# Loading q and k in runs of 18 tokens, sending five batches through DRAM rows, and reordering the front of a fused attention and MLP kernel

## The chip, the cores and the metric

The kernel runs on one core of one Trainium2 chip. The metric is the device time of one execution in microseconds, the lowest being best. Most executions of one kernel agree within some 0.3%, and some fall in a slower state; a run over 1.5% above the fastest of its kernel is called slow.

## The reference

Eight batches of eight heads attend within a window of 32 tokens to either side; the result, as 4608 tokens of 512 values, goes through two matrix products with an ELU between them.

```python
B, H, S, D = 8, 8, 576, 64
scores = (q @ k.T) / sqrt(D);  masked where |i - j| > 32
attn   = softmax(scores);      x = (attn @ v) as [B*S, H*D]     # 4608 x 512
h = x @ w_in                                                    # 512 x 2048
g = where(h > 0, h, exp(min(h, 0)) - 1)
out = g @ w_out                                                 # 2048 x 512, f32
```

## The kernel before

The MLP is cut into 18 tiles of 256 tokens with 8 steps each, 144 steps in all. A step is eight first-layer products, an exp on ScalarE, two VectorE operations, and, two steps later, four second-layer products. The attention of 36 pairs of query blocks is spread between these steps as tasks: pair i is computed some steps before the tile that needs it. The products of the scores take q and k with the head dimension on partitions; so each batch is loaded as f32, cast to bf16 and transposed.

```python
def load_qk(b, which, part):              # rows of 6 tokens a partition: 96 partitions
    ...
    nc.sync.dma_start(out=t[...].rearrange("p (h x) -> p h x", h=H),
                      in_=(q, k)[which][b, :, ...].rearrange("h (p j) d -> p h (j d)", j=nj))

def rotate_v(b, m0=0, m1=VS - 1):         # the copy of V shifted by 64 tokens: DMA
    nc.sync.dma_start(out=o[0:64, m0:m1], in_=e[64:128, m0:m1])
    nc.sync.dma_start(out=o[64:128, m0:m1], in_=e[0:64, m0 + 1:m1 + 1])

def transpose_rows(b, which):             # bf16 rows written to DRAM, read back transposed
    nc.sync.dma_start_transpose(out=keys_or_queries(b, which), in_=in_dram.pop((b, which)))

def x_dma(i):                             # attention result of pair i, transposed by DMA
    nc.sync.dma_start_transpose(out=xT_of(i), in_=x_st.rearrange("p h d -> p (h d)"))

# the plan, for batches 2 to 7 (k0: step at which the batch's first pair begins)
for b in range(2, B):
    k0 = begin[first_pair(b)]
    if b >= 3:
        kk = max(k0 - 26 if b < 5 else k0 - 36, 18)
        at(kk, "mid", load_qk, b, 0, WHOLE)
        at(kk + 1, "mid", load_qk, b, 1, WHOLE)
        ...                               # loads of V from step kk + 2
    if b < 5:                             # casts on GpSimd, transposes on TensorE
        for n in range(2 * HP):
            ...
            at(kk - 2 - b // 3, "mid", cast_qk, b, which, WHOLE, (hp,), nc.gpsimd)
            at(kk, "mid", transpose_qk, b, which, WHOLE, (hp,), nc.scalar)
    else:                                 # casts on ScalarE, rows through DRAM
        ...
        at(c0 + 6, "mid", write_rows, b, which)
        at(c0 + 9, "mid", transpose_rows, b, which)
    at(k0 - HALF, "mid", rotate_v, b)
```

SyncE issues its transfers in program order. In one queue stand the loads of q and k, the DMA transposes of the rows in DRAM, the DMA transposes of x, which the first-layer products wait for, and the stores of the result.

The softmax here doesn't subtract the row's maximum and nothing guards it: scores larger than these inputs give would overflow.

## Time and profile before

| | before |
|---|---|
| median of its first 3 runs | 337.37 us (336.4 to 337.61) |
| span of the profiled execution (slow) | 340.9 us |
| TensorE busy | 307.2 us, 90% |
| first MLP product starts | 26.3 us |
| GpSimd's casts of batch 2, VectorE stretched beside them | around 68 us |

The page of a profile gives busy time by engine and in forty slices of the span. The timeline lists start, length and, in brackets, the idle time ahead with what ended it. The prediction shows the lines.

### The profile page before, as it was taken

To read this page: it belongs to the slowest core of one execution; us is meant where nothing else is said; L and a number is where in the kernel's file an instruction comes from. 1 tells how busy PE (TensorE), PEld (TensorE's weight loads), DVE (VectorE), ACT (ScalarE), POOL (GpSimd) and SP (SyncE) were. 2 spreads that over 40 slices of the span, in tenths; PEclk is the share of its full clock that TensorE was granted. 3 is DMA by queue.
4 is the path that set the end of the run, shared out by engine and by line. 5 is a ranking of instruction groups with operands and counts; after the bars stand their busy time and mean duration, and the time that the engine had idled before them with its cause. 6 is when DMAs were issued, how large, how long until landed. Compare 5 with 4: busy or idle time off the path is not lost.

```text
span 340.9 us, 7736 instructions
## 1 busy us (share of the span) xinstructions
PE 307.2 (90%) x3152; PEld 203.3 (60%) x3152; DVE 239.8 (70%) x446; ACT 171.8 (50%) x262; POOL 63.4 (19%) x84
## 2 busy tenths in 40 slices
PE   0358999789899999899999999799999999999994
PEld 0245666456566666566666666556666666666661
DVE  4445667577786779676877778377777787877663
ACT  1624264555556634587646666446645444434431
POOL 8352310094461129110011100000000000000000
PEclk9999999899999999999999999979999999999998
DMA  8999999999999999918999999969590420202011
GB/s 174 183 231 219 216 164 200 211 228 228 148 149 169 234 198 188 174 67 165 221 250 176 203 245 158 215 104 223 95 200 18 139 74 22 77 17 80 0 62 62
DMA packets 93862, 52.72 MB, mean 155 GB/s; under 512 B 67908, under 2 KB 87364, under 8 KB 93828
## 3 DMA queue, kind: packets, MB, share of 16 engines
q1 hardware_dynamic: 51428, 39.79, 55.8%
q0 software_dynamic: 41728, 8.92, 38.9%
q10 hardware_dynamic: 672, 3.54, 3.4%
q8 instruction: 24, 0.39, 0.5%
q14 instruction: 10, 0.08, 0.1%
HBM read 36.70 MB, written 12.98 MB: 146 GB/s over the span
## 4 chain that ended last, share of the span: by engine, by line
PE 74%; DMA 12%; DVE 8%; ACT 3%; issue 1%; SPq 0%; DVEq 0%
PE ps L489 34%; PE psY L516 31%; DMA xT<-x_st 8%; PE psS L312 3%; PE psS L284 3%; PE ptx L265 3%; DMA f<-in_k_dram 2%; DVE g_sb L502 2%; DVE m_sb L497 2%; ACT e_sb L495 2%; DMA Vo<-Ve 2%; DVE x_st L324 1%; ACT qkb L211 1%; DVE pm L300 1%; ACT pu L291 1%
## 5 line engine op out<-in xcount | busy, mean ns | idle before, releaser
L495 ACT ACTIVATE e_sb<-ps 128x512 f32<-128x512 f32 x144 | 86.0, 597 | 148.4 <-PE ps L489 146.4
L489 PE MATMUL ps<-xT,w_in_sb 128*128 128x256 bf16 x1152 | 153.1, 277 | 5.8 <-DVE xT L346 3.7
L516 PE MATMUL psY<-w_out_sb,g_sb 128*128 128x512 bf16 x576 | 149.7, 383 | 0.9 <-DVE g_sb L502 0.9
L489 PEld LDWEIGHTS <-w_in_sb 128*128 128x128 bf16 x1152 | 111.3, 99 | 44.6 <-issue 6.7
L502 DVE SCALAR_TENSOR_TENSOR g_sb<-ps,m_sb 128x512 bf16<-128x512 f32 x144 | 99.3, 690 | 13.8 <-DVE m_sb L497 0.5
L497 DVE TENSOR_SCALAR m_sb<-e_sb 128x512 bf16<-128x512 f32 x144 | 66.0, 459 | 60.2 <-ACT e_sb L495 58.7
L516 PEld LDWEIGHTS <-g_sb 128*128 128x128 bf16 x576 | 52.9, 98 | 39.8 <-DVE g_sb L502 1.5
L123 POOL DMA_DIRECT2D Ve<-in_v_dram x40 | 34.1, 858 | 94.5 <-PE psS L312 81.0
L291 ACT ACTIVATE pu<-psS 128x1024 bf16<-128x1024 f32 x36 | 36.5, 1019 | 3.2 <-PE psS L284 3.1
L265 PE MATMUL ptx<-ident,qkb 96*128 96x96 bf16 x240 | 17.7, 221 | 14.4 <-DVE qkb L213 12.0
L324 DVE TENSOR_TENSOR x_st<-psS,rc 128x512 bf16<-128x512 f32 x36 | 24.9, 691 | 6.4 <-DMA xT<-x_st 5.2
L300 DVE TENSOR_TENSOR pm<-pu,masks 128x1024 bf16<-128x1024 bf16 x36 | 26.4, 733 | 2.0 <-ACT pu L291 1.7
L213 POOL CAST qkb<-f 96x768 bf16<-96x768 f32 x24 | 20.8, 901 | 31.6 <-DMA f<-in_q_dram 22.0
L265 PEld LDWEIGHTS <-qkb 96*128 96x128 bf16 x240 | 14.5, 106 | 16.4 <-DVE qkb L213 12.5
L312 PEld LDWEIGHTS <-pm 128*64 128x64 bf16 x576 | 12.8, 115 | 17.0 <-DVE pm L300 11.4
L243 ACT CAST rows<-f 96x768 bf16<-96x768 f32 x24 | 19.7, 822 | 0.0
L284 PE MATMUL psS<-qT,kT 64*128 64x64 bf16 x576 | 15.3, 196 | 3.2 <-DVE x_st L324 1.8
L284 PEld LDWEIGHTS <-kT 64*128 64x128 bf16 x576 | 11.2, 98 | 10.7 <-issue 7.3
L312 PE MATMUL psS<-Vo,pm 128*64 128x65 bf16 x256 | 14.8, 203 | 2.6 <-DMA Vo<-Ve 1.8
L312 PE MATMUL psS<-Ve,pm 128*64 128x65 bf16 x320 | 16.8, 202 | 0.0
L211 ACT COPY qT<-ptx 128x576 bf16<-128x576 bf16 (+1 forms) x18 | 12.4, 689 | 4.1 <-PE ptx L265 4.1
L525 DVE COPY y_sb<-psY 128x512 f32<-128x512 f32 x18 | 12.3, 683 | 2.8 <-PE psY L516 2.8
(29 smaller groups left out, 64.3 us busy)
## 6 DMA issues: line engine op xcount, KB each, us to landing
out_dram<-y_sb SPq DMA_DIRECT2D x18, 512.0 KB, 3.4
f<-in_q_dram SPq DMA_DIRECT2D x6, 1152.0 KB, 12.7
f<-in_k_dram SPq DMA_DIRECT2D x6, 1152.0 KB, 15.9
in_dram<-rows ACTq DMA_DIRECT2D x6, 576.0 KB, 4.2
Vo<-Ve SPq DMA_DIRECT2D x12, 260.0 KB, 5.3
Ve<-in_v_dram POOLq DMA_DIRECT2D x24, 128.0 KB, 13.2
f<-in_q_dram SPq DMA_DIRECT2D x4, 576.0 KB, 9.7
f<-in_k_dram SPq DMA_DIRECT2D x4, 576.0 KB, 11.7
```

What stands on the lines that cost most here:

```text
L123: nc.gpsimd.dma_start(out=V_e[b % 3][p0:p1, m, :, 0:D], in_=v[b, :, lo + p0:lo + p1, :].rearrange("h p d -> p h d"))
L265: nc.tensor.transpose(pt[:, g, j * SP_:(j + 1) * SP_], src[:, j, g * 128:(g + 1) * 128], ident[0:SP_, 0:SP_])
L284: nc.tensor.matmul(psS[:, h % 2, hp * 128 + z * QB:hp * 128 + (z + 1) * QB], lhsT=kT[b % 2][base:base + 64, KPAD + hp * S + QB * qb - WIN: ...
L291: nc.scalar.activation(pu, _bap(psS, [psS.ap[0], [1, 1024]]), AX.Exp, scale=SCALE)
L300: nc.vector.tensor_mul(pm, pu, _bap(mm, [mm.ap[0], [0, H], [1, 2 * QB]]))
L312: nc.tensor.matmul(psS[QB * z:QB * (z + 1), par, hp * VD:(hp + 1) * VD], lhsT=pm[:, par * HP + hp, z * QB:(z + 1) * QB], rhs=vv[:, qb // 2 ...
L324: nc.vector.tensor_mul(x_st, _bap(psS, [psS.ap[0], [VD, HP], [512, 2], [1, D]]), _bap(rc, [rc.ap[0], [2, HP], [1, 2], [0, D]]))
L489: nc.tensor.matmul(ps[:, j, :], lhsT=w_in_sb[:, do, fo * 128:(fo + 1) * 128], rhs=xT[t][:, :, do, :], start=(do == 0), stop=(do == NDO - 1))
L495: nc.scalar.activation(e_sb, ps, AX.Exp)
L497: nc.vector.tensor_scalar(m_sb, e_sb, -1.0, None, ALU.add)
L502: nc.vector.scalar_tensor_tensor(g_sb, psH.pop(kk), 0.0, m_t.pop(kk), ALU.max, ALU.min)
L516: nc.tensor.matmul(psY[t][ts], lhsT=g_sb[:, j, ts * 128:(ts + 1) * 128], rhs=w_out_sb[:, s * FG + j, :], start=(s == 0 and j == 0), stop=( ...
```

## The change

Its intent: longer contiguous rows for q and k (18 tokens, or 9 in the front, on 128 partitions), so fewer packets in those loads; batches 3 and 4 through DRAM too, so 96 transposes fewer on TensorE; no casts on GpSimd; the shifted copy of V by VectorE instead of DMA; a quicker front, with products of zeros in TensorE's waits to keep its clock up. The core of the diff, with cuts marked:

```diff
     def load_qk(b, which, part):
...
+        src = (q, k)[which][b, :, z * NC * nj:(z + 1) * NC * nj, :].rearrange(
+            "(g h) (c j) d -> c g h (j d)", h=2, j=nj)
+        for h in range(2):
+            nc.sync.dma_start(out=t[:, h, :], in_=src[:, :, h, :])
...
-        nc.sync.dma_start(out=o[0:64, m0:m1], in_=e[64:128, m0:m1])
-        nc.sync.dma_start(out=o[64:128, m0:m1], in_=e[0:64, m0 + 1:m1 + 1])
+        nc.vector.tensor_copy(o[0:64, m0:m1], e[64:128, m0:m1])
+        nc.vector.tensor_copy(o[64:128, m0:m1], e[0:64, m0 + 1:m1 + 1])
...
+    def idle(n, tag):
+        ps = ps_tile([128, 512], FP32, tag, "ps_idle")
+        for _ in range(n):
+            nc.tensor.matmul(ps, lhsT=zeros[:, 0:128], rhs=zeros,
+                             start=True, stop=True)
...
+    idle(12, "y1")
+    front_cast(0, HALF_A, nc.vector)
+    front_transpose(0, HALF_A, nc.scalar, ("h0", "h1"))
+    idle(5, "u")
+    front_cast(1, HALF_A, nc.scalar)
+    front_transpose(1, HALF_A, nc.vector, ("y0", "y1"))
     for i, tag in ((0, "s"), (1, "u")):
         scores(i, tag)
+    idle(8, "h1")
...
-    pair_at(4, 10)
-    pair_at(5, 13)
+    pair_at(4, 9)
+    pair_at(5, 12)
...
-            kk = max(k0 - 26 if b < 5 else k0 - 36, 18)
+            kk = max(k0 - 30, 18)
             at(kk, "mid", load_qk, b, 0, WHOLE)
             at(kk + 1, "mid", load_qk, b, 1, WHOLE)
...
-        if b < 5:
-            ...                              # casts on GpSimd, transposes on TensorE
+        if b == 2:
+            free = [f for f in range(17, k0) if f not in starts]
+            ...                              # casts on ScalarE, transposes on TensorE
         else:
+            free = [f for f in range(k0 - LEAD, k0) if f not in starts]     # LEAD = 18
+            for n, (which, j0) in enumerate(groups):
+                at(free[n], "end", cast_qk, b, which, WHOLE, j0, 6, nc.scalar)
+                if j0 == 12:
+                    at(free[n], "end", write_rows, b, which)
+                    at(free[n] + 4, "mid", transpose_rows, b, which)
-        at(k0 - HALF, "mid", rotate_v, b)
+        at(k0 - HALF - 1, "dve", rotate_v, b)
```

More of the change, by code (lines that the diff above doesn't have):

```diff
@@ L44 @@
     HP = H // 2
-    SJ = 6
-    SP_ = S // SJ
+    NC = 128 // HP
+    SJ = S // NC
     VS = 5
@@ L108, in load_qk @@
         z, nj = part
-        if (b, which) not in qk_f:
-            qk_f[b, which] = lpool.tile([SP_, H * SJ * D], FP32,
-                                        tag=f"f{which}", name=f"f{which}")
-        t = qk_f[b, which]
-        n = H * nj * D
-        nc.sync.dma_start(
-            out=t[:, z * n:(z + 1) * n].rearrange("p (h x) -> p h x", h=H),
-            in_=(q, k)[which][b, :, z * SP_ * nj:(z + 1) * SP_ * nj, :]
-            .rearrange("h (p j) d -> p h (j d)", j=nj))
+        t = lpool.tile([128, 2, nj * D], FP32, tag=f"f{which}{nj}",
+                       name=f"f{which}")
+        qk_f[b, which, z] = t
+        src = (q, k)[which][b, :, z * NC * nj:(z + 1) * NC * nj, :].rearrange(
+            "(g h) (c j) d -> c g h (j d)", h=2, j=nj)
+        for h in range(2):
+            nc.sync.dma_start(out=t[:, h, :], in_=src[:, :, h, :])
     def load_v(b, m):
@@ L155, in w_in_at @@
         return w_in_sb[0:1, 0, (c + 1) * (D_FF // 4) - 1:(c + 1) * (D_FF // 4)]
+    zeros = cpool.tile([128, 512], BF16, name="zeros")
+    nc.vector.memset(zeros, 0.0)
     for i in range(3):
@@ L171 @@
             load_qk(0, which, part)
-    for m in (1, 2, 0, 3, 4):
+    for m in (1, 0, 2, 3, 4):
         load_v(0, m)
-    rotate_v(0, 0, 2)
-    rotate_v(0, 2, VS - 1)
     load_w_in(0)
@@ L213, in copy_on, with cast_qk @@
             eng.tensor_copy(d_, s_)
-    def cast_qk(b, which, part, hps, eng):
+    def cast_qk(b, which, part, j0, n, eng):
         z, nj = part
-        hp0, nh = hps[0], 2 * len(hps)
-        n = H * nj * D
-        s_ = qk_f[b, which][:, z * n + 2 * hp0 * nj * D:
-                            z * n + (2 * hp0 + nh) * nj * D]
-        s_ = _bap(s_, [s_.ap[0], [nj * D, nh], [D, nj], [1, D]])
-        t = lpool.tile([SP_, nj, nh * D], BF16, tag=f"b{which}", name="qkb",
-                       bufs=4)
-        qk_b[b, which, z, hp0] = t
-        copy_on(eng, _bap(t, [t.ap[0], [D, nh], [nh * D, nj], [1, D]]), s_)
+        if (b, which, z) not in qk_b:
+            qk_b[b, which, z] = lpool.tile(
+                [128, nj, 2 * D], BF16, tag=f"b{which}{nj}", name="qkb")
+        t = qk_b[b, which, z]
+        copy_on(eng,
+                t[:, j0:j0 + n, :].rearrange("p j (h d) -> p h j d", h=2),
+                qk_f[b, which, z][:, :, j0 * D:(j0 + n) * D].rearrange(
+                    "p h (j d) -> p h j d", d=D))
     def keys_or_queries(b, which):
         if which == 0:
-            return qT[b % 2]
-        return kT[b % 2][:, KPAD:KPAD + HP * S].rearrange(
-            "p (g s) -> p g s", g=HP)
-    rows, in_dram = {}, {}
-    def cast_rows(b, which, hp):
-        if hp == 0:
-            rows[b, which] = lpool.tile([SP_, SJ, H * D], BF16,
-                                        tag=f"r{which}", name="rows", bufs=1)
-        n = SJ * D
-        s_ = qk_f[b, which][:, 2 * hp * n:(2 * hp + 2) * n]
-        d_ = rows[b, which][:, :, 2 * hp * D:(2 * hp + 2) * D]
-        nc.scalar.copy(
-            _bap(d_, [d_.ap[0], [D, 2], [H * D, SJ], [1, D]]),
-            _bap(s_, [s_.ap[0], [n, 2], [D, SJ], [1, D]]))
+            return qT[b % 2].rearrange("p g s -> p (g s)")
+        return kT[b % 2][:, KPAD:KPAD + HP * S]
+    in_dram = {}
     def write_rows(b, which):
-        t = dpool.tile([S, H * D], BF16, tag=f"d{which}", name="in_dram")
+        t = dpool.tile([HP * S, 2 * D], BF16, tag=f"d{which}", name="in_dram")
         in_dram[b, which] = t
         nc.scalar.dma_start(
-            out=t.rearrange("(p j) c -> p j c", j=SJ), in_=rows.pop((b, which)))
+            out=t.rearrange("(g c j) x -> c g (j x)", g=HP, j=SJ),
+            in_=qk_b.pop((b, which, 0)).rearrange("p j x -> p (j x)"))
     def transpose_rows(b, which):
@@ L255, in transpose_rows, with transpose_qk @@
             out=keys_or_queries(b, which), in_=in_dram.pop((b, which)))
-    def transpose_qk(b, which, part, hps, evac, tag="t0"):
+    def transpose_qk(b, which, part, j0, n, evac, tag="t0"):
         z, nj = part
-        src = qk_b.pop((b, which, z, hps[0]))
-        nh = len(hps)
-        W = 512 if nh > 1 else 1024
-        pt = ps_tile([128, nh, W], BF16, tag, "ptx")
-        for g in range(nh):
-            for j in range(nj):
-                nc.tensor.transpose(
-                    pt[:, g, j * SP_:(j + 1) * SP_],
-                    src[:, j, g * 128:(g + 1) * 128], ident[0:SP_, 0:SP_])
-        n = SP_ * nj
-        d = keys_or_queries(b, which)[:, hps[0]:hps[0] + nh, z * n:(z + 1) * n]
-        pitch = d.ap[1][0] if nh > 1 else n
+        src = qk_b[b, which, z]
+        pt = ps_tile([128, 1024 if n <= 8 else 2048], BF16, tag, "ptx")
+        for j in range(n):
+            nc.tensor.transpose(
+                pt[:, j * 128:(j + 1) * 128], src[:, j0 + j, :], ident)
+        d = keys_or_queries(b, which)
         copy_on(evac,
-                _bap(d, [d.ap[0], [pitch, nh], [nj, SP_], [1, nj]]),
-                _bap(pt, [pt.ap[0], [W, nh], [1, SP_], [SP_, nj]]))
+                _bap(d, [d.ap[0], [S, HP], [nj, NC], [1, n]],
+                     z * NC * nj + j0),
+                _bap(pt, [pt.ap[0], [1, HP], [HP, NC], [128, n]]))
     st = {}
@@ L343, in xT_of, with x_evac @@
         return xT[t][:, z, :, :]
-    def x_evac(i):
-        nc.vector.tensor_copy(xT_of(i), st.pop(i))
+    def x_evac(i, eng=nc.vector):
+        copy_on(eng, xT_of(i), st.pop(i))
     def x_dma(i):
@@ L354, in first_pair, with front_cast, front_transpose @@
         return NQB * b // 2
-    warm = cpool.tile([128, 1], FP32)
-    nc.vector.memset(warm, 0.0)
-    nc.scalar.activation(warm, warm, AX.Exp)
-    def front_qk(part, tags):
-        for g in range(2):
-            hps = (2 * g, 2 * g + 1)
-            cast_qk(0, 0, part, hps, nc.vector)
-            cast_qk(0, 1, part, hps, nc.scalar)
-            transpose_qk(0, 0, part, hps, nc.scalar, tags[g])
-            transpose_qk(0, 1, part, hps, nc.vector, tags[2 + g])
-    front_qk(HALF_A, ("h0", "h1", "y0", "y1"))
+    SPLIT = ((0, 5), (5, 4))
+    def front_cast(which, part, eng):
+        for j0, n in SPLIT:
+            cast_qk(0, which, part, j0, n, eng)
+    def front_transpose(which, part, evac, tags):
+        for (j0, n), tag in zip(SPLIT, tags):
+            transpose_qk(0, which, part, j0, n, evac, tag)
+    def idle(n, tag):
[3 more added lines that the diff above has]
+                             start=True, stop=True)
+    warm = cpool.tile([128, 1], FP32)
+    nc.scalar.activation(warm, zeros[:, 0:1], AX.Exp)
+    idle(12, "y1")
[4 more added lines that the diff above has]
+    front_transpose(1, HALF_A, nc.vector, ("y0", "y1"))
     for i, tag in ((0, "s"), (1, "u")):
         scores(i, tag)
+    idle(8, "h1")
+    front_cast(0, HALF_B, nc.vector)
+    front_transpose(0, HALF_B, nc.scalar, ("h0", "h1"))
     for i in (0, 1):
         mask(i)
-    front_qk(HALF_B, ("h0", "h1", "y0", "y1"))
-    for fn in (pv, normalize, x_transpose, x_evac):
-        for i in (0, 1):
-            fn(i)
+    front_cast(1, HALF_B, nc.scalar)
+    idle(4, "y1")
+    front_transpose(1, HALF_B, nc.scalar, ("y0", "y1"))
+    rotate_v(0, 0, 2)
+    idle(4, "h1")
+    for i in (0, 1):
+        pv(i)
+    for i in (0, 1):
+        normalize(i)
+    rotate_v(0, 2, VS - 1)
+    idle(4, "h1")
+    for i in (0, 1):
+        x_transpose(i)
+    for i in (0, 1):
+        x_evac(i, nc.scalar)
     gate(w_out_sb[0:1, NFO // 4 - 1, D_MODEL - 1:D_MODEL])
@@ L386 @@
         load_w_out(c)
-    rotate_v(1, 0, 2)
     gate(w_in_at(3))
@@ L392 @@
         load_v(1, m)
-    rotate_v(1, 2, VS - 1)
     for which in range(2):
@@ L422 @@
         at(1, "dve", mask, i)
-        at(1, "mid", pv, i)
+        at(1, "end", pv, i)
         at(2, "dve", normalize, i)
         at(2, "mid", x_transpose, i)
-        at(3, "dve", x_evac, i)
+        at(2, "end", x_evac, i, nc.scalar)
     at(4, "dve", swap_pools)
-    allh = tuple(range(HP))
     for part, kq in ((HALF_A, 8), (HALF_B, 16)):
         for which in range(2):
-            at(kq - 1, "mid", cast_qk, 1, which, part, allh,
+            at(kq - 1, "mid", cast_qk, 1, which, part, 0, SJ // 2,
                (nc.scalar, nc.vector)[which])
-            at(kq + which, "mid", transpose_qk, 1, which, part, allh,
+            at(kq + which, "mid", transpose_qk, 1, which, part, 0, SJ // 2,
                nc.scalar, "s")
-    pair_at(4, 10)
-    pair_at(5, 13)
+    at(10, "dve", rotate_v, 1, 0, 2)
+    at(17, "dve", rotate_v, 1, 2, VS - 1)
+    pair_at(4, 9)
+    pair_at(5, 12)
     pair_at(6, 18)
@@ L449 @@
         at(kk + 2, "end", x_dma, i)
+    starts = set(begin.values()) | {9, 12, 18}
+    LEAD = 18
     for b in range(2, B):
@@ L457 @@
                 at(kk + 2 + m // 3, "mid", load_v, b, m)
-        if b < 5:
-            for n in range(2 * HP):
-                which, hp = n // HP, n % HP
-                kk = k0 - (8 if b == 2 else 10) + n
-                at(kk - 2 - b // 3, "mid", cast_qk, b, which, WHOLE, (hp,),
-                   nc.gpsimd)
-                at(kk, "mid", transpose_qk, b, which, WHOLE, (hp,), nc.scalar)
-        else:
-            for which in range(2):
-                c0 = k0 - 27 + 8 * which
-                for hp in range(HP):
-                    at(c0 + (0, 1, 4, 5)[hp], "end", cast_rows, b, which, hp)
-                at(c0 + 6, "mid", write_rows, b, which)
-                at(c0 + 9, "mid", transpose_rows, b, which)
-        at(k0 - HALF, "mid", rotate_v, b)
+        groups = [(which, j0) for which in range(2) for j0 in (0, 6, 12)]
+        if b == 2:
+            free = [f for f in range(17, k0) if f not in starts]
+            for n, (which, j0) in enumerate(groups):
+                at(free[max(n - 1, 0)], "end", cast_qk, b, which, WHOLE, j0,
+                   6, nc.scalar)
+                at(free[n + 1], "mid", transpose_qk, b, which, WHOLE, j0,
+                   6, nc.scalar)
+        else:
+            free = [f for f in range(k0 - LEAD, k0) if f not in starts]
+            for n, (which, j0) in enumerate(groups):
+                at(free[n], "end", cast_qk, b, which, WHOLE, j0, 6, nc.scalar)
[3 more added lines that the diff above has]
+        at(k0 - HALF - 1, "dve", rotate_v, b)
     order = [(z, n) for z in range(2) for n in range(HALF)]
```

## The prediction

> **What bounds the kernel now.** I read the core's clock (0.987, one core, so no die to compare), then the page's busy shares and slices, then the timeline of the front, then TensorE's waits in windows of 10 us, then the queue of SyncE. The shares come first:
>
> ```profile
> PE 307.2 (90%) x3152; PEld 203.3 (60%) x3152; DVE 239.8 (70%) x446; ACT 171.8 (50%) x262; POOL 63.4 (19%) x84
> PE   0358999789899999899999999799999999999994
> ```
>
> TensorE is the bound, except in slices 1 to 4 (the front), slice 8 (60 to 68 us) and slice 27 (about 222 us). So there are two questions: what work leaves TensorE, and which holes close. The pace where nothing disturbs it, from the timeline near the end:
>
> ```profile
> 316.49 1.04 PE L489 MATMUL ps<-xT,w_in_sb 128*128 128x256 bf16 x8
> 318.23 1.04 PE L489 MATMUL ps<-xT,w_in_sb 128*128 128x256 bf16 x8
> ```
>
> One step (8 products of 256 columns, 4 of 512) starts every 1.737 us. From 230.91 to 238.79 us lie four steps and one attention pair: 7.88 - 4 x 1.737 = 0.93 us per pair. The chain of waits gives a group of six q/k transposes 0.26 us, so 43 ns each. My ledger of the span: front 26.3; 144 x 1.737 = 250.1; 34 pairs after the front x 0.93 = 31.6; 192 transposes after the front, about 9; transposes of x, 1.5; tail after the last product 340.9 - 336.15 = 4.75. Sum 323.3, so about 17.6 us of the 340.9 are holes. The front:
>
> ```profile
> 8.42 0.83 ACT L211 CAST qkb<-f 96x768 bf16<-96x768 f32 x1 [2.33 <-DMA f<-in_k_dram]
> ...
> 22.68 0.26 PE L312 MATMUL psS<-Vo,pm 128*64 128x65 bf16 x1 [1.84 <-DMA Vo<-Ve]
> ...
> 26.32 1.87 PE L489 MATMUL ps<-xT,w_in_sb 128*128 128x256 bf16 x8 [0.52 <-DVE xT L346]
> ...
> 29.09 1.89 PE L489 MATMUL ps<-xT,w_in_sb 128*128 128x256 bf16 x8
> ```
>
> See that k lands at 8.4 us, that the shifted copy of V, a DMA of 5.6 us, releases the second products at 22.68, and that the first MLP products take 1.87 us for the 0.87 of the steady state. The second-layer products begin at 34.99 (8.67 us later, of which only 4.5 is work, so 4.1 lost). Then slice 8:
>
> ```profile
> 64.50 1.03 PE L489 MATMUL ps<-xT,w_in_sb 128*128 128x256 bf16 x8 [1.86 <-DVE xT L346]
> 65.88 1.84 PE L516 MATMUL psY<-w_out_sb,g_sb 128*128 128x512 bf16 x4
> 67.51 1.91 PE L489 MATMUL ps<-xT,w_in_sb 128*128 128x256 bf16 x8
> 68.33 3.32 POOL L213 CAST qkb<-f 96x768 bf16<-96x768 f32 x4 [22.01 <-DMA f<-in_q_dram]
> 71.66 1.03 PE L489 MATMUL ps<-xT,w_in_sb 128*128 128x256 bf16 x8 [0.83 <-ACT y_sb L524]
> 73.36 1.04 DVE L497 TENSOR_SCALAR m_sb<-e_sb 128x512 bf16<-128x512 f32 x1 [1.20 <-ACT e_sb L495]
> ```
>
> A wait for xT behind VectorE's cast, then half pace, then GpSimd's casts with VectorE's 0.43 us operation stretched to 1.04. Counting products in windows, 60 to 90 us loses 6.3 us. SyncE's queue explains slice 27:
>
> ```profile
> 199.01 14.68 SPq L254 DMA_TRANSPOSE qT<-in_dram  x1
> 213.79 4.94 SPq L350 DMA_TRANSPOSE xT<-x_st  x2
> ```
>
> A DMA transpose issued right behind 2.4 MB of loads held the queue for 14.68 us; the transposes of x came behind it, and VectorE and TensorE waited (about 4 us lost; a like wait at 141 us cost 1.2). Named holes: 4.1 + 6.3 + 4 + 1.2 = 15.6.
>
> The profiled run took 343.73 us and is marked slow; 343.73 - 340.9 = 2.8 lies outside the span, so a usual run of 337.37 has a span near 334.5, 6.4 shorter. I choose to read the two waits behind DMA transposes (5.2 us) as mostly absent from usual runs; the trace can't prove it.
>
> **What the Trainium skill says.** (1) "TensorE: Matmul & The Clock Gate", the part on the clock gate: after an idle window of about 3.4 us the array runs at half clock until a busy one. The trace agrees in effect: 1.87 against 0.87 us behind the gappy front and after the hole at 62 us. The same page's part on PE-mode transpose says that transposes don't count as busy; no run here shows that yet. (2) "SBUF — State Buffer", Who interferes with whom: VectorE's two-port modes and GpSimd lock each other out. The trace agrees: 0.43 to 1.04 us. (3) "VectorE: DVE Perf Modes", the perf-mode tier table: a bf16 copy within SBUF runs at 4x, 693 ns for 2048 elements. The trace has no such copy yet; its f32 casts (560 ns for 768, 951 for 1536) have a slope of 0.51 ns an element, which is the 2x of that table. (4) "Perfetto Trace Analysis", DMA Optimizations: transfers under 2 KB have significant overhead each. Here 87364 of 93862 packets are under 2 KB; pieces of q and k are 768 or 1536 bytes before, 2304 or 4608 after.
>
> **The change part by part.**
>
> Loads. q and k of the first batch are 4 x 768 packets before, 4 x 256 after. They ran near 220 GB/s (2.36 MB from about 2 to 12 us); I take 350 for the longer rows, as the best slices of the later 1536-byte loads show 340 to 390. So q lands by 4.5, k by 6, the second halves by 9, and V, which ran mostly after them, by about 13 for its first three blocks instead of 16.4.
>
> Front, by the durations above, estimated on each engine's order. VectorE's fills end at 6.3 us (a zero tile of about 0.49 is added to the 5.85), q casts 0.49 + 0.43 to 7.3, its copies out on ScalarE 0.70 + 0.58 to 8.55, k casts 0.72 + 0.60 to 9.9, k's copies out on VectorE to 11.2, scores to 11.95, two exps to 13.6. Second halves on ScalarE: copies out 1.3, k casts 1.3, to 16.7; k's transposes to 16.95; four zero products 0.86 to 17.8; weighted V 0.86 to 18.7; the shifted V is now two VectorE copies of about 0.44 and is ready by 15.3. Normalising, transposing and copying x ends near 21.2. First MLP product at 21.2 instead of 26.3: **-5.1**. Zero products run in waits and should keep the clock up.
>
> First steps. At full clock the first three steps reach the second layer after about 7.3 us instead of 8.67 (exp, mask and normalise of pairs 2 and 3 still make it wait): **-1.4**.
>
> Transposes. Batches 3 and 4 go through DRAM: 96 transposes x 43 to 50 ns leave a TensorE-bound stretch: **-4.5**. Batches 1 and 2: 96 x 43 = 4.1 us become 72 of 128 columns, 72 x 57 = 4.1: nothing.
>
> Slice 8. GpSimd's 24 casts (20.8 us) go to ScalarE, which frees VectorE of the stretching, and pair 5 comes a step earlier, so xT is there in time: the 6.3 go. What comes: scores of pair 4 directly behind k's copy out in the same step, about 1.3; the 0.83 wait for y stays; ScalarE in steps 17 to 26 carries six casts and six copies of about 0.83, 1.0 us a step on top of 1.0, against TensorE's 2.25, so it is near full: 1.0 for jams. Net **-3.2**.
>
> Shifted V: 2 copies of 2080 elements x (693/2048) ns = 0.70 each, per batch 1.4 us in VectorE's emptiest step. VectorE gains 11 us in all and loses 7 of stretching; two steps of slack in the products hide it: 0.
>
> DRAM rows. Ten DMA transposes instead of six. The one that frightens me is q of batch 3: in program order it stands with the load of k of batch 4 just ahead of the transpose of x of pair 9, which is needed three steps later. Before, that transpose took 4.1 us of some 5 available. Behind an issue of 3 to 5 us and 1.2 MB more it must be late; 4 to 5 us of waiting and some half clock could follow. Later pairs have seven or eight steps of slack. I count **+3.5**.
>
> Sum: -5.1 - 1.4 - 4.5 - 3.2 + 3.5 = -10.7, so 326.7. By the new ledger: 21.2 + 250.1 + 31.6 + 4.1 + 1.5 + 4.75 = 313.3, holes 2.8 + 1.3 + 0.8 + 1.0 + 3.5 = 9.4, outside 2.8, so 325.5. I predict **325.5 us**.
>
> **The rivals.** (a) The queue of transposes bites: each DRAM transpose holds SyncE as at 199 us, and x comes late again and again: +8 to +12, some 335. For it: the 14.68. Against: the loads have a third of the packets and stand 16 steps ahead. (b) The weights become the front's bound: the first w_in quarter landed near 20.3 us and the second near 26.9, and the new order wants them at 21.2 and 25.9; if the small packets of V keep their pace, half of the front's gain turns into a wait: 328 to 330. (c) Batch 2's casts now stand in ScalarE's order eight us earlier than the data used to land (68.3); SyncE no longer waits for V in between, so I expect it near 55, but if not, exps stop behind the cast: +3 to +5. (d) No late x at all and a quicker front: 319 to 321.
>
> **Range and chances.** The gains of TensorE's own work and of the front are fairly firm (6 to 12 together); holes are not, by 4 either way. Range 318.5 to 332.5. 2% is 330.6: faster 0.80, within 2% 0.17, slower 0.03.
>
> **What would show it.** The first MLP product near 21 us, lasting about 1 us and not 1.87; GpSimd without casts and the 128x512 operation never above 0.6 us; 108 transposes on TensorE; VectorE copies of V near 0.7 us; a wait of the products on xT about step 32. I am wrong if the first product starts after 24 us, if V copies take 2 us, or if SyncE holds DRAM transposes over 10 us more than once.

## More of the kernel before

One view it didn't show is SyncE's queue around the transposes of x of pairs 8 and 9 in the kernel before:

```profile
95.38 8.59 SPq L350 DMA_TRANSPOSE xT<-x_st  x2
104.07 0.54 SPq L114 DMA_DIRECT2D f<-in_q_dram  x1
```

Here the load of q comes after those two transposes of x.

## The result, and the profile after

The changed kernel took 342.95 us (median of four runs, 342.27 to 343.44), the kernel before on the same chip 337.49 (336.4 to 338.02). The ratio is 1.0165, with a 95% interval from 1.0134 to 1.0195. Ratios here are the mean time of one kernel's fast runs over that of the other's in the same rounds, so not quite the ratio of the medians quoted. It is slower by 1.65%: clear of the noise, less than the 2% of the verdicts here ("same"), and outside the predicted range.

The page after, busy shares, slices and granted clock:

```profile
PE 309.8 (91%) x3057; PEld 199.3 (59%) x3057; DVE 243.0 (71%) x460; ACT 174.4 (51%) x262; POOL 43.3 (13%) x60
PE   7677989998963999999799999999999999999994
PEclk9799999999995999999799999999999999999999
```

Counted from 1, slices 1 to 4 are busier (partly with products of zeros) and slice 8 is 9 now. But there are two new holes: slices 12 and 13 (94 to 111 us) and slice 20 (162 to 170), and in slices 13 and 20 (and 2, in the front) the clock falls. The waits of TensorE on transfers name them (in total, times, longest, in us):

```profile
PE ps L501 <- DMA xT<-x_st: 9.7, 2, 9.3
PE psS L265 <- DMA kT<-in_dram: 2.2, 1, 2.2
```

The timeline of TensorE at both places:

```profile
108.10 1.89 PE L501 MATMUL ps<-xT,w_in_sb 128*128 128x256 bf16 x8 [9.28 <-DMA xT<-x_st]
109.78 1.87 PE L528 MATMUL psY<-w_out_sb,g_sb 128*128 128x512 bf16 x4
...
166.15 0.61 PE L265 MATMUL psS<-qT,kT 64*128 64x64 bf16 x16 [2.19 <-DMA kT<-in_dram]
166.69 1.89 PE L528 MATMUL psY<-w_out_sb,g_sb 128*128 128x512 bf16 x4
```

The products of step 32 wait 9.28 us for the transposed x of pair 9 and then run at half pace (1.89 for the usual 1.04). SyncE's queue shows what was ahead of that transpose:

```profile
87.86 2.60 SPq L331 DMA_TRANSPOSE xT<-x_st  x1
90.52 1.22 SPq L115 DMA_DIRECT2D f<-in_q_dram  x2
92.00 4.99 SPq L240 DMA_TRANSPOSE qT<-in_dram  x1
97.03 2.35 SPq L115 DMA_DIRECT2D f<-in_k_dram  x2
99.43 4.01 SPq L331 DMA_TRANSPOSE xT<-x_st  x2
```

Line 1 is pair 8's x. Then come the load of q of batch 4, the DRAM transpose of q of batch 3, the load of k of batch 4, and only at 99.43 pair 9's x (with pair 10's). The chain of work that ended last goes through the same transfers:

```profile
99.43 8.63 DMA xT<-x_st
108.10 1.89 PE ps L501 x8
...
143.41 13.16 DMA in_dram<-qkb
156.58 9.52 DMA kT<-in_dram
166.15 0.61 PE psS L265 x14
```

So the second hole is of the same kind: batch 4's rows took 13.16 us to be written to DRAM, with the loads of batch 5 issued just ahead of them, and 9.52 to come back.

The table below is taken from the traces: the stretch between the starts of the first-layer products of two steps, in us. "Before" is the profile of a fast run of the kernel before (the first experiment), as the one in the prediction was slow.

| stretch | before, fast | after | e12 | e10 |
|---|---|---|---|---|
| start to step 0 | 26.6 | 24.1 | 21.6 | 24.4 |
| steps 0 to 3 | 9.4 | 8.2 | 8.2 | 8.2 |
| 3 to 31 | 66.2 | 64.3 | 64.3 | 64.2 |
| 31 to 32 | 2.5 | 11.6 | 4.2 | 2.5 |
| 32 to 40 | 17.6 | 18.9 | 18.9 | 17.9 |
| 40 to 56 | 34.7 | 32.5 | 35.7 | 32.0 |
| 56 to 60 | 7.9 | 11.7 | 9.5 | 7.9 |
| 60 to 143 | 160.0 | 160.7 | 160.7 | 162.4 |
| 143 to the end | 8.8 | 8.8 | 8.8 | 8.5 |

At step 31 the changed kernel is 5.7 us ahead of the one before (it starts at 96.54 and not at 102.25). One step later it is 3.4 behind, and it gets back 2.2 only between 40 and 56. e12 and e10 are experiments below.

The front of the changed kernel: k's cast, the scores, the products of zeros, the first MLP product.

```profile
9.89 1.24 ACT L209 CAST qkb<-f 128x640 bf16<-128x640 f32 x2 [1.43 <-DMA f<-in_k_dram]
12.66 1.03 PE L265 MATMUL psS<-qT,kT 64*128 64x64 bf16 x32 [1.08 <-DVE kT L211]
13.63 3.00 PE L352 MATMUL ps_idle<-zeros 128*128 128x512 bf16 x8
24.07 1.03 PE L501 MATMUL ps<-xT,w_in_sb 128*128 128x256 bf16 x8 [0.67 <-ACT xT L209]
```

k lands at 9.89, 1.5 later than before, and not earlier. The scores then take 1.03 us for 32 products, and the eight zero products 3.00; where the clock holds they take 0.64 and 1.67 to 1.90 (below). The first MLP product is at full pace but starts at 24.07, not 21.2.

By a count of the trace's packets, the longer rows brought no faster load here: in the first 10 us q's and k's rows come to 1.74 MB in 755 packets, and before to 1.75 MB in 2278. Over the whole run their packets fell from 15360 to 5120, but those of the DRAM rows grew, and the total only fell from 93862 to 92455.

What came as predicted: no casts on GpSimd, and VectorE's 128x512 operation no longer stretched (429 ns mean; 459 before); VectorE's copies of V at 0.70 us each; 108 transposes on TensorE. In the groups, and for the copy in the timeline:

```profile
L509 DVE TENSOR_SCALAR m_sb<-e_sb 128x512 bf16<-128x512 f32 x144 | 61.8, 429 | 62.0 <-ACT e_sb L507 60.2
L248 PE MATMUL ptx<-ident,qkb 128*128 128x128 bf16 x108 | 8.9, 220 | 3.6 <-ACT qkb L209 3.0
...
115.79 0.70 DVE L127 COPY Vo<-Ve 64x2080 bf16<-64x2080 bf16 x1
```

### The profile page after: what moved, and what is told of

Its sections match the earlier page's. It is cut to its first block, busy times and chain, and to the rows that moved or that the text cites. A ratio compares the mean times of both kernels' runs of the same rounds, so it can differ in the third digit from the quotient of the medians.

```text
span 340.6 us, 7540 instructions
## 1 busy us (share of the span) xinstructions
PE 309.8 (91%) x3057; PEld 199.3 (59%) x3057; DVE 243.0 (71%) x460; ACT 174.4 (51%) x262; POOL 43.3 (13%) x60
## 4 chain that ended last, share of the span: by engine, by line
PE 73%; DMA 11%; DVE 8%; ACT 3%; issue 2%; SPq 1%; DVEq 0%; ACTq 0%
PE ps L501 32%; PE psY L528 31%; DMA in_dram<-qkb 4%; PE psS L265 3%; PE psS L293 3%; DMA kT<-in_dram 3%; DMA xT<-x_st 3%; DMA f<-in_k_dram 2%; DVE m_sb L509 2%; DVE g_sb L514 2%; ACT e_sb L507 2%; DVE x_st L305 1%; PE ptx L248 1%; PE ps_idle L352 1%; DVE Vo L128 1%
## 5 line engine op out<-in xcount | busy, mean ns | idle before, releaser
L501 PE MATMUL ps<-xT,w_in_sb 128*128 128x256 bf16 x1152 | 151.0, 275 | 12.3 <-DMA xT<-x_st 9.7
L509 DVE TENSOR_SCALAR m_sb<-e_sb 128x512 bf16<-128x512 f32 x144 | 61.8, 429 | 62.0 <-ACT e_sb L507 60.2
L209 ACT CAST qkb<-f 128x768 bf16<-128x768 f32 (+3 forms) x42 | 34.4, 832 | 1.4 <-DMA f<-in_k_dram 1.4
L281 DVE TENSOR_TENSOR pm<-pu,masks 128x1024 bf16<-128x1024 bf16 x36 | 24.6, 683 | 3.4 <-ACT pu L272 3.3
L293 PEld LDWEIGHTS <-pm 128*64 128x64 bf16 x576 | 12.0, 110 | 16.1 <-DVE pm L281 13.1
L265 PEld LDWEIGHTS <-kT 64*128 64x128 bf16 x576 | 11.0, 97 | 12.7 <-issue 6.7
L293 PE MATMUL psS<-Ve,pm 128*64 128x65 bf16 x320 | 15.9, 197 | 1.4 <-DVE pm L281 1.4
L352 PE MATMUL ps_idle<-zeros 128*128 128x512 bf16 x37 | 12.3, 486 | 1.3 <-DVE zeros L156 1.3
L248 PE MATMUL ptx<-ident,qkb 128*128 128x128 bf16 x108 | 8.9, 220 | 3.6 <-ACT qkb L209 3.0
L536 ACT COPY y_sb<-psY 128x512 f32<-128x512 f32 x18 | 10.5, 584 | 2.0 <-PE psY L528 2.0
L209 ACT COPY qT<-ptx 128x768 bf16<-128x768 bf16 (+3 forms) x9 | 7.4, 846 | 6.6 <-PE ptx L248 6.5
## 6 DMA issues: line engine op xcount, KB each, us to landing
Ve<-in_v_dram POOLq DMA_DIRECT2D x24, 128.0 KB, 11.5
```

The lines of the kernel that those rows point to most:

```text
L209: nc.scalar.copy(d_, s_)
L265: nc.tensor.matmul(psS[:, h % 2, hp * 128 + z * QB:hp * 128 + (z + 1) * QB], lhsT=kT[b % 2][base:base + 64, KPAD + hp * S + QB * qb - WIN: ...
L281: nc.vector.tensor_mul(pm, pu, _bap(mm, [mm.ap[0], [0, H], [1, 2 * QB]]))
L293: nc.tensor.matmul(psS[QB * z:QB * (z + 1), par, hp * VD:(hp + 1) * VD], lhsT=pm[:, par * HP + hp, z * QB:(z + 1) * QB], rhs=vv[:, qb // 2 ...
L501: nc.tensor.matmul(ps[:, j, :], lhsT=w_in_sb[:, do, fo * 128:(fo + 1) * 128], rhs=xT[t][:, :, do, :], start=(do == 0), stop=(do == NDO - 1))
L509: nc.vector.tensor_scalar(m_sb, e_sb, -1.0, None, ALU.add)
```

## The experiments

Theory O, the order: the x of pair 9 is late because large transfers stand just ahead of it in SyncE's queue. Rival T: DRAM transposes as such are what holds the queue. Rival C: the DRAM traffic is too much wherever it stands, and moving it moves the wait. In the texts recorded before e1 to e4, O is called A; C stands there as B (overloaded whatever the order) and as C (the wait moves to a later x). For the front: the clock, the late k, or nothing to gain. All kernels gave correct results; no run e7 is on record. Unless said otherwise the edits are to the changed kernel.

| label | edit | fast runs, us | ratio to before, 95% interval |
|---|---|---|---|
| e1_order | loads of batch 4 two steps later, DRAM transposes of batch 3 one | 334.53, 334.95, 339.1 | 0.9808 [0.9667, 0.9948] |
| e2_pe34 | batches 3 and 4 on TensorE | 333.65 to 334.47 | 0.9726 [0.9659, 0.9793] |
| e3_x89_pe | x of pairs 8, 9 on TensorE | 331.43 to 336.27 | 0.9712 [0.9622, 0.9802] |
| e4_pe34_loads | e2 and batch 4's loads later | 328.07 to 331.45 | 0.9814 [0.9758, 0.987] |
| e5_no_zeros | e4 without zero products | 328.45 to 328.94 | 0.9787 [0.9768, 0.9805] |
| e6_more_zeros | e4 with 12 instead of 5 in the wait for k | 328.15 to 328.7 | 0.9775 [0.9757, 0.9793] |
| e8_no_dram | e4, no batch through DRAM | 332.92 to 335.12 | 0.9944 [0.9903, 0.9984] |
| e9_v_copies | e6, V copies moved | 327.83 to 330.03 | 0.9757 [0.971, 0.9804] |
| e10_dram4 | e9, batch 4 through DRAM, loads of batch 5 later | 325.85 to 329.82 | 0.9678 [0.9632, 0.9724] |
| e11_v_later | e6, V and the weights held until k's first half has landed | 327.75 to 328.2 | 0.9732 [0.9694, 0.9771] |
| e12_loads_only | batch 4's loads two steps later | 329.59, 331.83, 333.57 | 0.9845 [0.9774, 0.9915] |

In e0 to e3 the kernel before fell mostly in the slow state: two fast runs, 336.81 and 340.99. Those ratios are loose.

### The kernel before, once more

> The kernel before, once more, for a profile in the fast state (the one in hand was marked slow, 343.7 us against a usual 337.4). Expected: 337.5 us, ratio 1.00. If my reading of its ledger is right (waits behind DMA transposes at 140 and 212 to 230 us are mostly absent from usual runs), this profile shows neither hole or only small ones, and a span near 334.5. If instead they are part of every run, they are there again and the 6 us are elsewhere.

One fast run, the profiled one: 336.16 us with a span of 333.7; three slow ones. The wait near 222 us that the prediction had taken as absent from usual runs is absent (steps 80 to 90: 19.2 us, and 23.5 in the slow profile). That reading held. (SyncE still held the DRAM transpose at 195.85 us for 13.59 us there: a long hold alone does not make a wait.) But steps 3 to 31, which hold slice 8, take 66.2 us here and 68.3 in the slow profile: 2.1 us of the hole that I wanted to see closed was not in usual runs either.

### Both transfers moved out of the way

```diff
-            kk = max(k0 - 30, 18)
+            kk = 30 if b == 4 else max(k0 - 30, 18)
-                    at(free[n] + 4, "mid", transpose_rows, b, which)
+                    at(free[n] + (5 if b == 3 else 4), "mid",
+                       transpose_rows, b, which)
```

> The changed kernel with one thing different: the DRAM transpose of q of batch 3 and of k one step later (30 and 34 instead of 29 and 33), and the loads of batch 4 two steps later (30, 31 instead of 28, 29), so that in the order of SyncE the transpose of x of pair 9 comes before them. Theory A (the order in SyncE's queue makes x of pair 9 late: 9.28 us of waiting, then 8 + 4 products at half clock, about 1.9): the wait at step 32 goes, 343 - 11 = 332. Rival B (the DMA rings are overloaded there, so x is late whatever the order): most of the wait stays, 339 to 342. Rival C (the lateness moves to the next x, of pair 11, wanted at step 40): 337 to 340, with a wait at step 40.

The wait at step 32 is gone (steps 31 to 32: 2.2 us). But two others came, at step 39 on kT and at step 56 on x; TensorE's timeline, then the queue:

```profile
116.70 0.39 PE L265 MATMUL psS<-qT,kT 64*128 64x64 bf16 x8 [3.81 <-DMA kT<-in_dram]
154.64 1.87 PE L502 MATMUL ps<-xT,w_in_sb 128*128 128x256 bf16 x8 [3.35 <-DMA xT<-x_st]
```

```profile
102.34 9.09 SPq L240 DMA_TRANSPOSE kT<-in_dram  x1
111.48 2.85 SPq L331 DMA_TRANSPOSE xT<-x_st  x2
...
135.31 7.72 SPq L240 DMA_TRANSPOSE qT<-in_dram  x1
143.13 2.32 SPq L331 DMA_TRANSPOSE xT<-x_st  x1
```

O holds for step 32, and part of C with it: a DRAM transpose issued 4.9 us after 1.2 MB of loads (97.43) held the queue 9.09 us and was itself late.

### The DRAM transposes of batches 3 and 4 taken away

```diff
-        if b == 2:
-            free = [f for f in range(17, k0) if f not in starts]
+        if b < 5:
+            free = [f for f in range(k0 - 10, k0) if f not in starts]
```

> The changed kernel with batches 3 and 4 transposed on TensorE as batch 2 is (casts and copies out on ScalarE), so only three batches go through DRAM as before. Theory A: both waits that DRAM rows brought go (11 at step 32, and about 3.8 around 166 us where k of batch 4 was late), 72 transposes of 0.055 come back (4.0): 343 - 15 + 4 = 332. Rival D (ScalarE becomes the bound where it carries 12 more casts' worth of copies): 335 to 338. Rival B has no say here.

The hole at 166 us is gone. At step 32 a wait remains, with the loads of batch 4 still ahead of pair 9's x:

```profile
101.22 1.67 PE L501 MATMUL ps<-xT,w_in_sb 128*128 128x256 bf16 x8 [2.37 <-DMA xT<-x_st]
```

2.37 instead of 9.28. So the loads alone are not enough for the whole wait.

### The loads of batch 4 moved, the DRAM transpose left

This is the counterpart, one line of the change. (Batch 4's loads of V, on GpSimd's queue, move with it, here and in e1 and e4.)

```diff
-            kk = max(k0 - 30, 18)
+            kk = 30 if b == 4 else max(k0 - 30, 18)
```

> The changed kernel with one line altered: the loads of batch 4 at steps 30 and 31, behind the transpose of x of pair 9 in SyncE's order; the DRAM transpose of q of batch 3 stays just ahead of it. If the loads (1.2 MB) made that transpose late, the wait of 9.28 us at step 32 falls to 3 or less and the time to about 335 or 336. If the DRAM transpose ahead of it did, the wait stays above 6 us and the time above 340. The wait for kT near step 60 (2.19 us) is untouched in both.

```profile
89.46 1.95 SPq L240 DMA_TRANSPOSE qT<-in_dram  x1
91.71 1.61 SPq L331 DMA_TRANSPOSE xT<-x_st  x1
93.37 1.90 SPq L115 DMA_DIRECT2D f<-in_q_dram  x2
95.31 1.29 SPq L115 DMA_DIRECT2D f<-in_k_dram  x2
```

```profile
98.33 1.70 PE L501 MATMUL ps<-xT,w_in_sb 128*128 128x256 bf16 x8 [1.97 <-DMA xT<-x_st]
...
152.89 1.63 PE L501 MATMUL ps<-xT,w_in_sb 128*128 128x256 bf16 x8 [3.60 <-DMA xT<-x_st]
```

The wait falls to 1.97 us, as the first alternative said, and the fast runs are 329.59 to 333.57, all better than the 335 to 336 expected. The DRAM transpose held SyncE 1.95 us, where with a load just ahead of it it held 4.99. Together with e2 this settles the size: **each of the two causes alone leaves about 2 us of wait, as part of it falls into the slack between x's making and its use; both together leave 9.28.** They did more than add: counted from the start of step 31, pair 9's x lands after 0.3 us with neither (e4, below), 4.9 with the loads alone (e2), 4.2 with the DRAM transpose alone (e12, where the moved loads follow right behind x and may have a share) and 11.5 with both. So 4.6 and 3.9 alone became 11.2 together; the longer hold of SyncE, 4.99 for 1.95, is about as large as the excess. The second hole was not untouched as I had expected: in this profile it became a wait of 3.60 us for x at step 56.

### The victim moved instead

```diff
-        at(kk + 2, "end", x_dma, i)
+        if i < 10:
+            at(kk + 2, "end", x_transpose, i)
+            at(kk + 3, "dve", x_evac, i)
+        else:
+            at(kk + 2, "end", x_dma, i)
```

> The changed kernel with x of pairs 8 and 9 transposed on TensorE and copied out by VectorE, as for pairs 4 to 7, instead of by DMA; the DRAM rows stay as they are. Theory A and rival B both: the wait at step 32 goes, 332 to 333 (8 more products of 0.055 are 0.4). Rival C: the wait turns up at step 40 for pair 11: 337 to 340. Together with the run on the order: if this one gains 10 and that one doesn't, the rings and not the order are to blame.

With x of pairs 8 and 9 transposed by TensorE the wait at step 32 is gone; one is left, of 2.76 us for x at step 56. That the loss at step 32 goes with x's path through SyncE's queue is shown from a third side.

### Neither DRAM rows for batches 3 and 4 nor early loads

Edits of e2 and e12 together.

> The run with batches 3 and 4 on TensorE, and besides that the loads of q and k of batch 4 two steps later (30, 31). That run still waited 2.37 us at step 32 and lost 5 us with the half clock after it, although no DRAM transpose stood there: the loads of batch 4 (issued at 89 and 90 us) were just ahead of the transposes of x. Theory A in its wider form (whatever large transfer stands ahead of a small urgent one in the queue makes it late): the wait at step 32 goes too, 334 - 5 = 329, and no wait of TensorE on a DMA over 1 us is left. Rival B (rings overloaded whatever the order): 332 to 334.

329.57 us median; the waits of TensorE have no DMA among them any more. A hit. Pair 9's x is now issued ahead of the loads, as in the kernel before:

```profile
87.21 7.37 SPq L331 DMA_TRANSPOSE xT<-x_st  x2
94.64 1.23 SPq L115 DMA_DIRECT2D f<-in_q_dram  x2
95.91 1.25 SPq L115 DMA_DIRECT2D f<-in_k_dram  x2
```

### No zero products, and more of them

On e4: `idle()` returns at once; or `idle(12, "u")` for `idle(5, "u")`.

> The same as the run with the later loads, without any product of zeros. Theory Z (they hold the clock up): first MLP product not earlier than 23, the scores of the first pairs take 1.03 us and not 0.64, the first MLP products 1.87 and not 1.05: 2 to 3 us slower than that run. Rival Y (they do nothing, the front is bound by k's landing and ScalarE): within 0.7 us of it.

> The same as the run with the later loads, with 12 instead of 5 products of zeros in the wait for k. In the changed kernel's profile the scores at 12.66 us and the 8 zero products after them ran at half clock (3.00 us against 1.67 in the run on the order, where k landed 0.75 us sooner). Theory Z: with 12 the clock holds in every run, first MLP product at 21.5 to 22.5 in each profile, 0.5 to 1 us faster on average than with 5. Rival Y: no change, or later by the 0.5 us that the zero products may hold k's transposes.

Without zeros, TensorE runs the front at half pace, but the first product starts early:

```profile
21.63 1.87 PE L502 MATMUL ps<-xT,w_in_sb 128*128 128x256 bf16 x8 [0.67 <-ACT xT L209]
```

Step 3 is at 31.0 us, against 31.6 in e4 and 30.4 in e6; the medians are 328.9, 329.57, 328.38. So no gain from the change's own dose of zeros is shown, and my 2 to 3 us for e5 missed. With twelve in the wait for k the clock held in the profiled run:

```profile
12.24 0.64 PE L265 MATMUL psS<-qT,kT 64*128 64x64 bf16 x32 [1.08 <-DVE kT L211]
13.04 1.67 PE L352 MATMUL ps_idle<-zeros 128*128 128x512 bf16 x7 [0.16 <-issue]
```

All profiled runs that have these zeros, by when k's first cast starts and by whether the pace broke after it (scores above 0.64 us, or the seven or eight zero products after them 2.42 us and longer):

| zeros in that wait | k's cast starts | pace after it | first MLP product |
|---|---|---|---|
| 5 (e12, e1) | 8.93, 9.14 | held | 21.6, 21.8 |
| 5 (e3) | 9.48 | held | 22.2 |
| 5 (e4, e8) | 9.42, 9.44 | broke | 23.4, 23.8 |
| 5 (e2, after) | 9.60, 9.89 | broke | 23.9, 24.1 |
| 12 (e9, e6) | 9.09, 9.47 | held | 21.8, 22.2 |
| 12 (e10) | 10.18 | broke | 24.4 |
| 12 (e11, V held back) | 8.45 | held | 21.8 |

Where the pace holds, the first product comes 12.7 us after k's cast (13.3 in e11); where it breaks, 14.0 to 14.4. If it breaks, the zero products themselves run slowly, and the work behind them waits. That is how a filler costs time.

When k lands does not decide it alone: with five zeros 9.42 broke and 9.48 held. The clock records in the traces show more. In all five broken profiles the clock halves 6.83 us after it first became full, for 3.41 us: from 12.49 to 15.90 in the changed kernel, where it had become full at 5.66. With five zeros the pace broke where it became full between 4.84 and 6.23, and held between 6.40 and 7.15. So this moment, which varies though the first zeros start at 1.26 us in each, divides the seven cases; that it is the cause was not tested.

### V held back

```diff
+    nc.gpsimd.tensor_copy(v_gate, qk_f[0, 1, 0][0:1, 1, 0:1])   # waits for k's first half
     for m in (1, 0, 2, 3, 4):
         load_v(0, m)
```

> The fastest kernel so far (twelve zero products in the wait for k), with GpSimd's loads of V and of the weights held until k's first half of batch 0 has landed, by a one-element copy on GpSimd. Theory P (k lands at 9.5 us, not at the 6 that I predicted, because the packets of V share the DMA engines): q's cast starts before 6.0, k's at 6.5 to 7.5 instead of 9.47, and scores near 10. Rival L (the loads of q and k are limited by themselves, by their issue and their latency): k's cast still starts at 9 us or later. The end of the front may not gain, as the weights and V come later; time 326 to 332.

```profile
8.41 0.17 POOL L173 COPY v_gate<-f 1x1 f32<-1x1 f32 x1 [7.04 <-DMA f<-in_k_dram]
8.45 1.24 ACT L211 CAST qkb<-f 128x640 bf16<-128x640 f32 x2
```

k landed at 8.41 instead of 9.47 in e6. In the eleven profiles of the changed front with V beside it k's cast starts between 8.93 and 10.18, so V costs k some 0.5 to 1.8 us; but k lands no earlier than in the kernel before (8.42) even with no V beside it. Neither theory had the number: most of the way to my 6 us was missing for another reason than V. One candidate is untested: when k landed, 1.8 MB of q's and k's rows were under way, by a count of packets, and the first halves are 1.18 MB, so the second halves already had a share. The first product came at 21.8 (22.2 in e6): an earlier k would not have helped, as ScalarE copies q out until 8.45.

### How much the DRAM rows are worth

On e4, `b < 8` for `b < 5`: every batch on TensorE.

> The same as the run with the later loads, with all batches from 2 on transposed on TensorE, none through DRAM. If TensorE's pace is what the rest of the run is bound by, three more batches cost 3 x 36 x 0.055 = 5.9 us: 335. If the DMA traffic of the DRAM rows costs as much as they save, it is the same, 329 to 330.

334.1 us median, 4.5 above e4, where 5.9 had been expected. Batches 5 to 7 through DRAM pay.

### V's copies moved

```diff
-        at(k0 - HALF - 1, "dve", rotate_v, b)
+        if b == 2:
+            at(24, "mid", rotate_v, b)
+        else:
+            at(k0 - HALF + (1 if b == 3 else -1), "dve", rotate_v, b)
```

> The fastest kernel so far (batches 2 to 4 transposed on TensorE, loads of batch 4 at steps 30 and 31, twelve zero products in the wait for k), with VectorE's copies of V moved: batch 2's from step 22 to step 24, batch 3's two steps later. Theory V: the products of step 24 wait 1.1 us for xT because VectorE does the two 0.70 us copies of V just ahead of it; with them moved the wait goes and 327 to 327.5 us result, against 328.4. Rival: the copies then hold up the mask and the sums of the steps they move into, and nothing is gained: 328 to 329.

328.5 us: nothing gained. Step 24 starts 0.8 us earlier than in e6 (0.3 of it from the front), step 26 only 0.2, since the mask now waits behind the copies (steps 24 to 26: 5.3 us for 4.7). The rival's case.

### Batch 4 through DRAM again, with room ahead

```diff
-            kk = 30 if b == 4 else max(k0 - 30, 18)
+            kk = {4: 30, 5: 52}.get(b, max(k0 - 30, 18))
-        if b < 5:
+        if b < 4:                                     # batches on TensorE
-            free = [f for f in range(k0 - LEAD, k0) if f not in starts]
+            free = [f for f in range(k0 - (16 if b == 5 else LEAD), k0) if f not in starts]
```

> The same, with batch 4 through DRAM rows again, and the loads of batch 5 at steps 52 and 53, behind both DRAM transposes of batch 4. Theory O (what makes a small transfer late is the large one issued ahead of it on SyncE): no product waits for a DMA near step 56, TensorE loses 24 groups of transposes, and the time falls by about 2 us, to some 325.5. Rival C (the DRAM traffic itself makes it late, wherever it stands): a wait for xT or kT of 2 to 5 us between steps 52 and 64, 328 to 331 us.

326.36 us median of five: the fastest of all, 3.2% below the kernel before, and faster than e9 in the same rounds by 2.1. No wait near step 56. SyncE's queue there:

```profile
130.34 2.46 SPq L240 DMA_TRANSPOSE qT<-in_dram  x1
135.08 1.23 SPq L331 DMA_TRANSPOSE xT<-x_st  x1
138.03 0.37 SPq L541 DMA_DIRECT2D out_dram<-y_sb  x1
138.50 4.38 SPq L240 DMA_TRANSPOSE kT<-in_dram  x1
142.93 1.24 SPq L115 DMA_DIRECT2D f<-in_q_dram  x2
```

Both DRAM transposes stand ahead of the next loads. (The profiled run was the slowest of the five: a front of 24.4 and a wait of 1.28 us for kT of a later batch at 187 us.)

## Why the prediction was wrong

The time rose where it was predicted to fall, because one term of the sum was more than four times too small, and two were too hopeful. Measured numbers are from the table of stretches, after less before (fast).

| term | predicted | measured |
|---|---|---|
| front | -5.1 | -2.6 |
| first steps | -1.4 | -1.2 |
| transposes of batches 3 and 4 | -4.5 | about -4.3 |
| slice 8 and its neighbours (3 to 31) | -3.2 | about -1.4 |
| late x of pair 9, and other DRAM rows | +3.5 | about +15.7 |

The measured terms add up to 6.2; the spans differ by 6.9 (340.6 less 333.7), and steps 60 to 143 have the other 0.7. Batch 3's 48 transposes that are gone are worth 2.1 us at 43 ns each, worked out and not measured; by the trace 36 of them (1.5) stood in steps 31 to 40 and 12 (0.5) before. The fifth row: steps 31 to 40 take 20.1 us before, less 1.5, so about 18.5, and 30.4 after: 11.9 lost. Steps 56 to 60 lose 3.8. The fourth row is 2.0 less those 0.5. The third row is the 2.1 and the 2.2 between steps 40 and 56; e6 against e10 (batch 4 on TensorE or in DRAM) gives 2.0 for steps 40 to 60.

**"I count +3.5".** This is the step that failed. The place, the transfers and the step number were right: the wait came at step 32, behind q of batch 3 and the load of k of batch 4. I put it at 4 to 5 us, from an issue of 3 to 5 and 1.2 MB more, and then counted less. It was 9.28, and the half pace behind it took the loss to about 11.9. The terms named there came to more already: besides the issue of 3 to 5, 1.2 MB at the 220 to 350 GB/s of the same text is 3.4 to 5.4 us (an estimate), less 0.9 of slack. And the two delays did more than add: e2 and e12 show 4.6 and 3.9 us for each alone, 11.2 together, with the slack subtracted once.

**"Later pairs have seven or eight steps of slack".** In the changed kernel's profile that was nearly enough for x (one more wait, of 0.43 us), though in e1, e3 and e12 x came 2.8 to 3.6 us late at step 56. It says nothing of kT of batch 4, whose rows had a write of 13.16 us and a transpose of 9.52 in series. The nearest rival was (a), "x comes late again and again: +8 to +12": right in kind, but its reason was not seen. SyncE held no DRAM transpose for 10 us: the longest of the ten took 6.77. That stated alarm would have missed this.

**The front.** The first product came at 24.1, not 21.2. The order on the engines was read correctly: with the pace held it starts at 21.6 to 22.2. Here another stated alarm, a first product after 24 us, did ring. What failed is "I take 350 for the longer rows", so k by 6: it landed at 9.89, and e11 gives 8.41 even with V held. The 340 to 390 behind it seem to be what all queues moved together in single microseconds; in the kernel before q's and k's own 1536-byte rows never pass 297 in one. In the profiled run the pace then broke, worth some 1.5 us (14.2 against 12.7 after k's cast). "Zero products run in waits and should keep the clock up" did not hold in every run. (The 0.87 that the prediction sets beside 1.87 is half a step; its lines show 1.04 for the same eight products. The half pace stands.)

**Slice 8.** It went as intended, but 2.1 us of its hole belonged to the slow profile alone. I allowed for that at 141 and 222 us, not here.

Rivals (b) and (c) did not occur: weights set no wait in the front, and ScalarE's casts of batch 2 waited for no load. Of the 17.4 us between 325.5 and 342.95, the late transfers account for 12.2, the front and the first steps for 2.7, slice 8 for 1.8; the rest is unassigned. With the late transfers repaired, e10 gives 326.36, near 325.5, but with batch 3 on TensorE, twelve zeros and other places for loads and copies: that the two are near is partly luck. Whether all five batches can go through DRAM without a wait was not found.

**What the skill's pages contributed.** "VectorE: DVE Perf Modes" on the bf16 copy: 0.70 us measured for 2080 elements, as worked out. "TensorE: Matmul & The Clock Gate", Part 4: PE-mode transpose, says that transpose mode doesn't count as PE-busy the same way: in the changed front TensorE did only nine transposes between the end of the five zero products near 8.6 us and the scores at 12.66, and those ran at 1.03 instead of 0.64. That fits, though an idle wait would do the same, so it is not separated. The Trainium skill's "DMA: Bandwidth & Descriptors", Queues, rings and completion order, says that each engine takes turns between the queues that have work, a packet at a time. By my count from the trace, V's queue moved 462 packets in the first 10 us before and 1986 after, when q's and k's rows had grown; and holding V brought k in 1.06 us earlier (8.41 against 9.47, one profile each). This fits the page, if the trace's packets are what the page calls packets, which isn't known; the larger part of the lateness it does not explain.

## What to carry to other kernels

When several kinds of transfer share one issuing queue, list for each urgent small one everything issued in the steps ahead of it, add their times, and compare the sum with its slack once; they can do more than add (4.6 and 3.9 us alone, 11.2 together). A large load that isn't urgent goes behind it, and behind any DRAM transpose. Here two steps' delay of one batch's loads brought the ratio from 1.0165 to 0.9845, with no work removed. Before filling TensorE's waits with spare products, look at several profiles: here the pace held in some and broke in others of the same front, and where it breaks the fillers hold up the work.

## What the Trainium skill lacked or had wrong

- "DMA: Bandwidth & Descriptors", Latency and other measured facts, has 261 GB/s for a DMA transpose with a non-contiguous middle dimension (and more for a contiguous one): at most 2.3 us as an estimate for the 589,824 bytes of one batch's q or k. In these runs it took 9.52 us from issue to landing in the chain of the changed kernel, beside other loads. The page has no figure for a transpose that shares the engines with other transfers.
- The same page has sequencer cycles for a DMA transpose only in a table on a newer chip, and nothing on how the time for which it keeps the issuing sequencer grows with what stands ahead of it, which matters as later transfers wait for it: for the same transfer of q of batch 3, 1.95 us with x's transposes ahead (e12), 4.99 with a load just ahead (changed kernel); for k of batch 3 issued 4.9 us after 1.2 MB of loads, 9.09 (e1).
- "TensorE: Matmul & The Clock Gate" has nothing on products of zeros as fillers. They did hold the pace (scores 0.64 instead of 1.03 us), but a batch of seven or eight of them took 1.67 to 1.90 us where it held and 2.42 to 3.15 where it had broken.
